# The second product of a two-layer squared-relu network by Strassen's seven products, on pairs of token chunks

## The chip, the cores and the metric

The kernel runs on one core of a Trainium2 chip. A core has five engines with their own instruction queues: TensorE (PE in the profile, its weight loads PEld), VectorE (DVE), ScalarE (ACT), GpSimd (POOL) and SyncE (SP), which here only issues transfers. TensorE writes to PSUM, and VectorE and ScalarE read it from there. The metric is the device time of one execution in microseconds.

## The reference, cut to what matters

```python
B, H, S, D = (4, 8, 768, 64)
for t in range(S):
    state = gamma * state + einsum('bhd,bhe->bhde', k[:, :, t], v[:, :, t])
    y[:, :, t] = scale * einsum('bhd,bhde->bhe', q[:, :, t], state)
x = y.transpose(0, 2, 1, 3).reshape(3072, 512)
h = np.maximum(x @ w_in, 0.0)          # w_in 512 x 2048
out = (h * h @ w_out).astype(np.float32)   # w_out 2048 x 512
```
A recurrent attention with one decay per head gives 3072 tokens of 512 values. A network with a hidden width of 2048 follows: a product, a relu, a square, a second product. Inputs and output are fp32 in memory; the products take bf16 operands and add up in fp32.

## The kernel before, in words

The 3072 tokens are 24 chunks of 128. The attention takes chunk after chunk; a "visit" on TensorE (lines 686 to 723) has the small products of one chunk, VectorE brings its result to `xt` (L788), and the state is added up by VectorE (L779). Inputs are loaded by SP in order (L616), k and q are cast by GpSimd for most chunks (L421), v is scaled on VectorE (L627), and from chunk 7 on q and k are transposed by a DMA (L660). Four load buffers, six bf16 buffers for k, q and v (`NBF`), six for the transposed q and k (`NQT`) and four groups of four chunks for x (`NXT`) stand between the steps.

The first product, `ffn1`, works on blocks of one, two or four chunks (`BLOCKS`). A group of matmuls fills one PSUM bank of 512 columns (L835): x moves and w_in is the stationary operand, so the moving width is 128 times the number of chunks of the block. A relu on ScalarE brings the bank to `h2` in bf16 (L840), and VectorE squares it there, in place (L845).

The second product, `ffn2`, takes one chunk at a time: 16 matmuls with 128x128 of `h2` as the stationary operand and 512 columns of w_out moving add up in one bank (L880), ScalarE copies the bank to `osb` (L888), and SP stores 256 KB (L893). The last chunk is cut into 256, 128 and 128 columns (`LAST`), the last of them stored from ScalarE's queue.

There are four PSUM banks (`fps`) for both products. Two of them at most may be held by open groups of the second product.

The order of all this is not written by hand. Each operation is added to a planner (`Plan`) with its engine, an expected duration, what it reads and writes, and a priority; the planner places at every step the operation that can start first, the lower priority number first among equals, and each engine then executes its own instructions in that fixed order. An operation given a choice of engines goes where it can start first. The hardware waits only for the semaphores that follow from what is read and written; an engine whose next instruction is not ready waits, even if a later one is. `HOME` pins some casts to an engine. The second product of a chunk is offered once the first product is four chunks ahead (`F2WAIT`), with a priority some chunks later (`F2LAG`):

```python
while done2 < done and blk0[done] - blk0[done2] >= F2WAIT:
    ffn2(done2)
    done2 += 1
```

Of the kernel before, what the change touches and what calls it, by code (L numbers as in the profile page):

```python
# [18 lines left out]
class Plan:  # L19
# [18 lines left out]
        self.lastw = {}  # L38
        self.readers = {}

    def add(self, name, eng, dur, reads=(), writes=(), fn=None, prio=0.0, lat=0.0, bank=None, after=(), count=0):
# [22 lines left out]
        self.ops.append(dict(i=i, name=name, eng=eng, flex=flex, deps=sorted(deps), fn=fn,  # L64
                             prio=prio, lat=lat, bank=bank, count=count))
        return i

    def schedule(self, nbanks, max_open):
        ops = self.ops
        n = len(ops)  # L70
        users = [[] for _ in range(n)]
# [15 lines left out]
        if "PE" in eng_free:  # L87
            eng_free["PE"] = 0.06 * PRE
        bank_free = [0.0] * nbanks
        bank_of = {}  # L90
        open_groups = set()
        closed = {}
# [6 lines left out]
        while done < n:  # L99
            best = None  # L100
            for eng, cand in pool.items():
                ef = eng_free[eng]
                for i in cand:
                    o = ops[i]
                    t = max(ef, ready_at[i])
                    b = o["bank"]
                    if b is not None and b[0] == "open":
                        if b[2] and len(open_groups) >= max_open:
                            continue
                        free = [x for x in bank_free if x is not None]  # L110
                        if not free:
# [85 lines left out]
                    open_groups.discard(b[1])  # L197
            if b is not None:
                o["bank_index"] = bank_of[b[1]]
            done += 1  # L200
            for u in users[i]:
                same = list(ops[u]["eng"]) == [eng] and not move
# [11 lines left out]
TURN = (0.60, 1.10, 16, 2.4)  # L214
WIDE = (0.60, 2.80, 33, 0.6)
STORE = (0.30, 0.80, 9, 0.6)
BLOCKS = [2, 2, 1, 1, 2, 2, 2, 2, 2, 4, 4]
SPLIT = 6
AHEAD = 4
WARM = 20.0  # L220
# [19 lines left out]
WPRIO = {"in": -2.0, "out": 2.0}  # L240


HOME = {'cq7': 'DVE', 'cwin1.0': 'ACT', 'Eq0.1': 'ACT', 'cwin5.2': 'POOL', 'Ek0.0': 'ACT', 'cwin4.1': 'DVE', 'ck0.1': 'POOL', 'Eq2.0': 'DVE', 'cq0.0': 'DVE', 'cwout3.1': 'ACT', 'Eq0.0': 'ACT', 'cwout2.1': 'ACT', 'cwin4.2': 'DVE', 'cwout2.2': 'ACT', 'cq5': 'POOL', 'cwin4.0': 'DVE', 'cwout3.0': 'DVE', 'cwin0.0': 'ACT', 'cwout0.3': 'POOL', 'cwout1.0': 'DVE', 'cwout2.3': 'POOL'}
ROUND = []
RANK = {}
# [13 lines left out]
def kernel(  # L259
# [29 lines left out]
    blk0 = [sum(blocks[:i]) for i in range(NB)]  # L289
    for x, n in zip(blk0, blocks):  # L290
        assert 512 % (n * C) == 0 and x // 4 == (x + n - 1) // 4
    NLD, NBF, NQT, NXT, NH2, NWS, NOSB, NST = 4, 6, 6, 4, 3, 4, 3, 6
    NBANK = 4

    const = ctx.enter_context(tc.tile_pool(name="const", bufs=1))
# [521 lines left out]
    def ffn1(blk):  # L817
        nb = blocks[blk]
        n = nb * C
        per = 512 // n  # L820
        g, u0 = divmod(blk0[blk], 4)
        xt, h2, cols = xts[g % NXT], h2s[g % NH2], slice(u0 * C, u0 * C + n)
        for f0 in range(0, NFB, per):
            grp = ("f1", blk, f0)
            j = f0 // 4
            reads = [f"xt{g % NXT}.{u0 + u}" for u in range(nb)] + [
                f"win{j}.{cb}.{h}" for cb in range(NCB) for h in sorted({(f0 + u) % 4 // 2 for u in range(per)})]
            o1 = {}

            def mm(f0=f0, j=j, o1=o1):  # L830
                ps = fps[o1["op"]["bank_index"]]
                for u in range(per):
                    c = (f0 + u) % 4
                    for cb in range(NCB):
                        nc.tensor.matmul(ps[:, u * n : u * n + n], lhsT=w_in_bf[j][:, cb, c * P : (c + 1) * P],  # L835
                                         rhs=xt[:, cb, cols], start=(cb == 0), stop=(cb == NCB - 1))

            def relu(f0=f0, o1=o1):
                ps = fps[o1["op"]["bank_index"]]
                nc.scalar.activation(h2[:, f0 : f0 + per, cols],  # L840
                                     ps[:].rearrange("p (u n) -> p u n", u=per), AF.Relu)

            def square(f0=f0):
                hv = h2[:, f0 : f0 + per, cols]
                nc.vector.tensor_mul(hv, hv, hv)  # L845

            i0 = pl.add(f"F1.{blk}.{f0}", "PE", per * NCB * (n * 0.4167 + 3) / 1e3, reads, (f"g{grp}",), mm,
                        prio=blk0[blk] * 8 + 2 * f0 * nb / 4, lat=0.2, bank=("open", grp, False),
                        count=per * NCB)
            o1["op"] = pl.ops[i0]  # L850
            hk = [f"h{g % NH2}.{u0 + w}.{f0 + u}" for u in range(per) for w in range(nb)]
            pl.add(f"R{blk}.{f0}", "ACT", 0.6, (f"g{grp}",), hk, relu,
                   prio=blk0[blk] + f0 / 16 * nb, bank=("close", grp),
                   after=twin_users if g == NH2 - 1 else pt_users if g == 1 else ())
            pl.add(f"Q{blk}.{f0}", "DVE", 0.43, hk, hk, square, prio=blk0[blk] + f0 / 16 * nb + 2)

    def rows(m):
        return where(m)[0] * S + where(m)[1] * C

    def ffn2(blk):  # L860
        for q4 in range(blk0[blk], blk0[blk] + blocks[blk]):
            g, u = divmod(q4, 4)
            h2 = h2s[g % NH2]
            slot = q4 % NOSB
# [34 lines left out]
    for kind in pieces:  # L899
        for n in range(len(pieces[kind])):  # L900
            weights(kind, n)
    done = done2 = 0
    for m in range(-1, NM):
        n = m + 1
# [12 lines left out]
            visit(m, n if n < NM else None, t)  # L917
        while done < NB and blk0[done] + blocks[done] - 1 == m:
            ffn1(done)
            while done2 < done and blk0[done] - blk0[done2] >= F2WAIT:  # L920
                ffn2(done2)
                done2 += 1
            done += 1
    for blk in range(done2, NB):
        ffn2(blk)

    sequence = pl.schedule(NBANK, 2)
    if tc is not None:
        with tc.manual_schedule():
            one = nc.const_aps.tensor(1.0, [P, 1], BF16)  # L930
# [39 lines left out]
```

## Time and profile before

| what | value |
|---|---|
| time, median of 3 runs | 209.82 us (209.39 to 210.51) |
| span of the profiled execution | 207.7 us; the page gives no other time for it |
| TensorE busy | 198.5 us, 96% |
| VectorE / ScalarE / GpSimd busy | 112.1 / 88.9 / 44.2 us |
| first product's matmuls, share of the chain | 41% |
| second product's matmuls, share of the chain | 39% |
| relu L840, 96 of them | 597 ns each |
| square L845, 96 of them | 448 ns mean |
| copy of the second product L888, 512 columns | 597 ns |

The page's span runs from the first to the last instruction; the time of a run is some 2 us longer. Busy times of different engines overlap. A line of the second part stands for 40 equal slices of the span, and a digit for tenths of a slice. The chain is followed back from the last instruction, and its shares add up to the span. In the lists of instructions a line gives the line of the code, the engine, the operation, what is written and read, and how often; some matmul records can be missing, so counts of matmuls come from the code. A matmul's own duration includes the way through the array and overlaps the next one, so its cost is read from the distance between starts.

### The profile page before, as it was taken

The numbers are of one execution on the slowest core, as the hardware profiler recorded it, in microseconds if no ns is written. First come the engines' busy times: TensorE is split into PE (matmuls) and PEld (weight loads), VectorE is DVE, ScalarE is ACT, GpSimd is POOL, SyncE is SP. The second block draws the span as 40 slices with busy tenths as digits, with TensorE's granted clock in tenths as the row PEclk, the third lists the DMA queues.
The fourth block names the chain that finished last, engine by engine and source line by source line (L and its number), as shares of the span: only waits on it lengthen the run. The fifth ranks groups of instructions, "written<-read, shape, count | busy, mean of one in ns | idle before, by whom it ended". The sixth has DMA issues, their size and how long they took to land.

```text
span 207.7 us, 6150 instructions
## 1 busy us (share of the span) xinstructions
PE 198.5 (96%) x2666; PEld 126.0 (61%) x2691; DVE 112.1 (54%) x245; ACT 88.9 (43%) x149; POOL 44.2 (21%) x75
## 2 busy tenths in 40 slices
PE   7898999999999999999999999999999999999994
PEld 5555797754854866868578666554444444444454
DVE  2597598753664574867558838436575414222000
ACT  8454576644321633535325252313643226344121
POOL 6643344342211122312212222112200000000000
PEclk9997999999999999999999999999999999999999
DMA  6999999999999999999999999989940111011112
GB/s 164 290 318 320 349 338 317 379 212 221 219 243 199 200 253 164 200 237 235 160 224 209 159 246 216 146 189 205 215 104 0 54 50 54 0 50 52 50 54 101
DMA packets 95643, 38.41 MB, mean 185 GB/s; under 512 B 81024, under 2 KB 89600, under 8 KB 95616
## 3 DMA queue, kind: packets, MB, share of 16 engines
q1 hardware_dynamic: 95472, 37.95, 86.3%
q8 instruction: 21, 0.34, 0.7%
q10 hardware_dynamic: 144, 0.07, 0.1%
q14 instruction: 6, 0.05, 0.1%
HBM read 27.26 MB, written 6.29 MB: 162 GB/s over the span
## 4 chain that ended last, share of the span: by engine, by line
PE 89%; DMA 4%; SPq 4%; issue 2%; ACT 0%
PE fps L835 41%; PE fps L880 39%; DMA wst<-in_moe_w_in_dram 4%; SPq L436 4%; PE yy L686 2%; PE yy L701 2%; PE sc L723 1%; PE sc L712 1%; PE fps L669 0%; ACT w_in L417 0%; PE sc L522 0%; PE sc L533 0%; PE yy L642 0%; PE yy L522 0%; PE yy L533 0%
## 5 line engine op out<-in xcount | busy, mean ns | idle before, releaser
L835 PE MATMUL fps<-xt,w_in 128*128 128x256 bf16 (+2 forms) x703 | 92.5, 284 | 1.0 <-ACT w_in L417 0.9
L880 PE MATMUL fps<-w_out,h 128*128 128x512 bf16 (+2 forms) x392 | 86.6, 362 | 2.5 <-issue 1.9
L840 ACT ACTIVATE h<-fps 128x512 bf16<-128x512 f32 x96 | 57.3, 597 | 60.3 <-PE fps L835 56.7
L835 PEld LDWEIGHTS <-w_in 128*128 128x128 bf16 x704 | 63.3, 98 | 25.2 <-ACT w_in L417 1.1
L845 DVE TENSOR_TENSOR h<-h 128x512 bf16<-128x512 bf16 x96 | 42.0, 448 | 48.0 <-ACT h L840 47.8
L880 PEld LDWEIGHTS <-h 128*128 128x128 bf16 x416 | 38.1, 98 | 37.4
L888 ACT ACTIVATE osb<-fps 128x512 f32<-128x512 f32 (+2 forms) x26 | 14.7, 564 | 46.4 <-PE fps L880 43.5
L421 POOL CAST kqs<-kn 128x512 bf16<-128x512 f32 x20 | 13.2, 658 | 61.7 <-DMA kn<-in_k_dram 60.2
L788 DVE TENSOR_TENSOR xt<-yy,yf 128x512 bf16<-128x512 f32 x20 | 13.7, 686 | 15.0 <-PE yy L701 15.0
L627 DVE TENSOR_TENSOR vs<-vn,vf 128x512 bf16<-128x512 f32 x20 | 14.5, 727 | 6.2 <-DMA vn<-in_v_dram 6.2
L421 POOL CAST kqs<-qn 128x512 bf16<-128x512 f32 x19 | 12.8, 673 | 21.4 <-DMA qn<-in_q_dram 21.4
L779 DVE TENSOR_TENSOR state<-sc,state 128x256 bf16<-128x256 f32 x33 | 13.8, 418 | 0.6
L766 DVE TENSOR_TENSOR pt<-sc,cmask 128x512 bf16<-128x512 f32 x20 | 13.6, 680 | 0.3 <-PE sc L723 0.3
L701 PE MATMUL yy<-qkT,state 64*64 64x64 bf16 x296 | 9.9, 198 | 0.2
L686 PEld LDWEIGHTS <-vs 64*64 64x64 bf16 x320 | 4.2, 107 | 7.0 <-issue 6.6
L936 PE MATMUL fps<-ident 128*128 128x256 bf16 x31 | 7.3, 377 | 0.3 <-POOL ident L352 0.3
L421 POOL CAST w_in<-wst 128x512 bf16<-128x512 f32 x7 | 4.7, 681 | 8.9 <-DMA wst<-in_moe_w_in_dram 8.9
L686 PE MATMUL yy<-pt,vs 64*64 64x64 bf16 x320 | 6.4, 198 | 0.0
L701 PEld LDWEIGHTS <-state 64*64 64x64 bf16 x296 | 6.1, 107 | 0.4 <-PE yy L701 0.4
L723 PE MATMUL sc<-vs,kqs 64*64 64x64 bf16 x288 | 6.2, 193 | 0.0
L712 PE MATMUL sc<-qkT 64*64 64x64 bf16 x320 | 6.2, 193 | 0.0
L421 POOL CAST w_out<-wst 128x512 bf16<-128x512 f32 x7 | 4.4, 653 | 7.6 <-DMA wst<-in_moe_w_out_dram 7.6
(67 smaller groups left out, 85.0 us busy)
## 6 DMA issues: line engine op xcount, KB each, us to landing
out_dram<-osb SPq DMA_DIRECT2D x23, 256.0 KB, 3.7
qn<-in_q_dram SPq DMA_DIRECT2D x20, 256.0 KB, 5.0
kn<-in_k_dram SPq DMA_DIRECT2D x20, 256.0 KB, 5.1
vn<-in_v_dram SPq DMA_DIRECT2D x20, 256.0 KB, 4.9
wst<-in_moe_w_out_dram SPq DMA_DIRECT2D x4, 1024.0 KB, 10.1
wst<-in_moe_w_in_dram SPq DMA_DIRECT2D x4, 512.0 KB, 8.7
wst<-in_moe_w_in_dram SPq DMA_DIRECT2D x2, 1024.0 KB, 8.8
kn<-in_k_dram SPq DMA_DIRECT2D x2, 512.0 KB, 5.7
```

Source lines behind the costliest of these rows:

```text
L421: nc.gpsimd.tensor_copy(o, t)
L627: lambda: nc.vector.tensor_tensor(out=o[:], in0=t.rearrange("s (h d) -> s h d", h=H), in1=vf[:, i, :, None].to_broadcast([P, H, D]), op=AL ...
L686: nc.tensor.matmul(yy[L * c : L * c + L, sub, p * L : p * L + L], lhsT=vs[r, 4 * a + j, :], rhs=pt[r, a, j, :], start=(p == 0), stop=True, ...
L701: nc.tensor.matmul(yy[L * c : L * c + L, sub, p * L : p * L + L], lhsT=st[r, j, :], rhs=qkT[r, 1, j, sub * L : sub * L + L], start=False, ...
L766: lambda: nc.vector.tensor_tensor(out=pt[:], in0=sc[:, :, 0:256].rearrange("s g (p t) -> s g p t", p=NJ), in1=cmask[:, None, None, :].to_b ...
L779: f = lambda cc=cc, j1=j1, j0=j0: nc.vector.tensor_tensor(out=sts[j1][:], in0=cc, in1=sts[j0][:], op=ALU.add)
L788: lambda: nc.vector.tensor_tensor(out=xt[:, :, u * C : u * C + C].rearrange("s p (g t) -> s g p t", g=2), in0=yy[:, :, 0:256].rearrange("s ...
L835: nc.tensor.matmul(ps[:, u * n : u * n + n], lhsT=w_in_bf[j][:, cb, c * P : (c + 1) * P], rhs=xt[:, cb, cols], start=(cb == 0), stop=(cb = ...
L840: nc.scalar.activation(h2[:, f0 : f0 + per, cols], ps[:].rearrange("p (u n) -> p u n", u=per), AF.Relu)
L845: nc.vector.tensor_mul(hv, hv, hv)
L880: nc.tensor.matmul(ps[:, 0:w], lhsT=h2[:, fb, u * C : u * C + C], rhs=w_out_bf[j][:, c, ns], start=(fb == 0), stop=(fb == NFB - 1))
L888: lambda o1=o1, slot=slot, ns=ns, w=w: nc.scalar.activation(osbs[slot][:, ns], fps[o1["op"]["bank_index"]][:, 0:w], AF.Copy),
```

## The change

From chunk 4 on the second product works on pairs of chunks. With A the pair's squared h cut into 2 x 2 blocks (rows: the two chunks; columns: halves of the hidden width) and B = w_out cut into 2 x 2 (halves of the hidden width; 256 output columns each), the seven products of Strassen's rule stand in place of eight:

- M1 = (A11 + A22)(B11 + B22), M2 = (A21 + A22) B11, M3 = A11 (B12 - B22), M4 = A22 (B21 - B11), M5 = (A11 + A12) B22, M6 = (A21 - A11)(B11 + B12), M7 = (A12 - A22)(B21 + B22)
- C11 = M1 + M4 - M5 + M7, C12 = M3 + M5, C21 = M2 + M4, C22 = M1 - M2 + M3 + M6

Each product is eight matmuls of 256 columns. The order on TensorE is 3, 4, 1, 5, 2, 6, 7, in two PSUM banks A and B. The five sums of A (S1, S5, S2, S6, S7, 128x1024 in bf16) are made by VectorE; S6 and S7 overwrite blocks of `h2`, the others lie in the buffers where the weights were staged. The sums of B (T1, T3, T4, T6, T7, ten halves) are made once, by VectorE or GpSimd, in the same buffers. After products 3 and 4 ScalarE copies bank A (`e34`), which gives M3 and M4; products 5 and 2 then add to that bank, which gives C12 and C21, and ScalarE copies it again (`cc`). ScalarE copies M1 out of bank B (`e1`). Three additions in fp32, by GpSimd or VectorE (`t1`, `u1`, `w`), bring these together, and one addition by VectorE with bank B (`c`) gives C11 and C22. SP issues two stores of 256 KB for a pair.

The relu now writes fp32 into one of two buffers (`rts`, `NR`), and the square reads it there and writes bf16 to `h2`, on VectorE or ScalarE, whichever can start first; the planner has the two buffers as slots. `BLOCKS` has twos where it ended with two fours. `NBF` and `NQT` go from six to five, `NXT` from four to three. Chunks 0 to 3 keep the second product as it was; the split of the last chunk isn't met any more, since `UNTIL` is 24. In the planner the two new arguments `slot` and `nslots` do for the relu buffers what `bank` does for PSUM banks.

```diff
--- before.py
+++ after.py
...
-BLOCKS = [2, 2, 1, 1, 2, 2, 2, 2, 2, 4, 4]
+BLOCKS = [2, 2, 1, 1, 2, 2, 2, 2, 2, 2, 2, 2, 2]
...
+SQUARE = {"DVE": 0.7, "ACT": 0.63}
+WSUM = {"DVE": 0.72, "POOL": 2.6}
+ASUM = {"DVE": 0.72}
+FADD = {"POOL": 0.75, "DVE": 0.43}
+FADD2 = {"POOL": 1.3, "DVE": 0.7}
+FIRST, UNTIL = 4, 24
+PAIRS_B = {"T1": ((0, 0), (1, 1), ALU.add), "T3": ((0, 1), (1, 1), ALU.subtract), "T4": ((1, 0), (0, 0), ALU.subtract),
+           "T6": ((0, 0), (0, 1), ALU.add), "T7": ((1, 0), (1, 1), ALU.add)}
+PAIRS_A = {"S1": ((0, 0), (1, 1), ALU.add, None), "S5": ((0, 0), (0, 1), ALU.add, None),
+           "S2": ((1, 0), (1, 1), ALU.add, None), "S6": ((1, 0), (0, 0), ALU.subtract, (1, 0)),
+           "S7": ((0, 1), (1, 1), ALU.subtract, (0, 1))}
...
-    NLD, NBF, NQT, NXT, NH2, NWS, NOSB, NST = 4, 6, 6, 4, 3, 4, 3, 6
+    NLD, NBF, NQT, NXT, NH2, NWS, NOSB, NST = 4, 5, 5, 3, 3, 4, 3, 6
+    NR, NUN = 2, 2
...
+    rts = [sb(f"r{j}", [P, 512], FP32) for j in range(NR)]
+    e34s = [sb(f"e34{j}", [P, 512], FP32) for j in range(NUN)]
+    ccs = [osbs[j] for j in range(2)]
+    wus = [osbs[2], sb("wu", [P, DM], FP32)]
+    half_slots = [wst[j][:].rearrange("p a n -> p (a n)").bitcast(BF16).rearrange("p (s c n) -> p s c n", s=4, c=4)
+                  for j in range(4)]
...
-            def relu(f0=f0, o1=o1):
-                ps = fps[o1["op"]["bank_index"]]
-                nc.scalar.activation(h2[:, f0 : f0 + per, cols],
-                                     ps[:].rearrange("p (u n) -> p u n", u=per), AF.Relu)
-
-            def square(f0=f0):
-                hv = h2[:, f0 : f0 + per, cols]
-                nc.vector.tensor_mul(hv, hv, hv)
+
+            def relu(o1=o1):
+                nc.scalar.activation(rts[o1["relu"]["slot_index"]][:], fps[o1["op"]["bank_index"]][:], AF.Relu)
+
+            def square(on, f0=f0, o1=o1):
+                hv, rv = h2[:, f0 : f0 + per, cols], rts[o1["relu"]["slot_index"]][:].rearrange("p (u n) -> p u n", u=per)
+                if on == "ACT":
+                    nc.scalar.activation(hv, rv, AF.Square)
+                else:
+                    (nc.vector if on == "DVE" else nc.gpsimd).tensor_tensor(out=hv, in0=rv, in1=rv, op=ALU.mult)
 
...
-            pl.add(f"R{blk}.{f0}", "ACT", 0.6, (f"g{grp}",), hk, relu,
-                   prio=blk0[blk] + f0 / 16 * nb, bank=("close", grp),
+            i0 = pl.add(f"R{blk}.{f0}", "ACT", 0.6, (f"g{grp}",), (f"r{grp}",), relu,
+                        prio=blk0[blk] + f0 / 16 * nb, bank=("close", grp), slot=("open", grp))
+            o1["relu"] = pl.ops[i0]
+            pl.add(f"Q{blk}.{f0}", SQUARE, 0, (f"r{grp}",), hk, square, prio=blk0[blk] + f0 / 16 * nb + 2, slot=("close", grp),
                    after=twin_users if g == NH2 - 1 else pt_users if g == 1 else ())
-            pl.add(f"Q{blk}.{f0}", "DVE", 0.43, hk, hk, square, prio=blk0[blk] + f0 / 16 * nb + 2)
 
...
+    def sums_of_weights():
+        slot = [0]
+
+        def place():
+            j, s = divmod(slot[0], 4)
+            slot[0] += 1
+            return half_slots[j][:, s], [f"wst{j}.0", f"wst{j}.1"]
+        made = {}
+        for name, (x, y, op) in PAIRS_B.items():
+            for half in range(2):
+                t, held = place()
+                blocks_ = [w_out_bf[2 * r + half][:, :, 256 * c : 256 * c + 256] for r, c in (x, y)]
+                reads = [f"wout{2 * r + half}.{c}.{h}" for r, _ in (x, y) for c in range(4) for h in range(2)]
+                pl.add(f"W{name}.{half}", WSUM, 0, reads, [f"T{name}.{half}"] + held,
+                       lambda on, t=t, blocks_=blocks_, op=op: (nc.vector if on == "DVE" else nc.gpsimd).tensor_tensor(
+                           out=t, in0=blocks_[0], in1=blocks_[1], op=op), prio=3.0)
+                made[name, half] = (t, f"T{name}.{half}")
+        sums = {}
+        for j in range(NUN):
+            for name in ("S1", "S2", "S5"):
+                t, held = place()
+                sums[name, j] = (t.rearrange("p c (e n) -> p (c e) n", e=2), held)
+        return made, sums
+
+    def products(c0):
+        n = units_made[0]
+        units_made[0] += 1
+        g, u = divmod(c0, 4)
+        h2 = h2s[g % NH2]
+        z = n % NUN
+        a = {(r, c): h2[:, 8 * c : 8 * c + 8, (u + r) * C : (u + r + 1) * C] for r in range(2) for c in range(2)}
+        key = {(r, c): [f"h{g % NH2}.{u + r}.{f}" for f in range(8 * c, 8 * c + 8)] for r in range(2) for c in range(2)}
+        for name, (x, y, op, dst) in PAIRS_A.items():
+            if dst is None:
+                a[name], held = asums[name, z]
+                key[name] = [f"{name}.{z}"]
+            else:
+                a[name], held, key[name] = a[dst], [], key[dst]
+            pl.add(f"{name}.{c0}", ASUM, 0, key[x] + key[y], key[name] + held,
+                   lambda on, o=a[name], x=a[x], y=a[y], op=op: (nc.vector if on == "DVE" else nc.gpsimd).tensor_tensor(
+                       out=o, in0=x, in1=y, op=op), prio=c0 + 1.5)
+        wb = lambda r, c, f: w_out_bf[2 * r + f // 4][:, f % 4, 256 * c : 256 * c + 256]
+        bkey = lambda r: [f"wout{2 * r + x}.{c}.{h}" for x in range(2) for c in range(4) for h in range(2)]
+        tb = lambda name, f: wsums[name, f // 4][0][:, f % 4]
+        tkey = lambda name: [wsums[name, x][1] for x in range(2)]
+        PRODUCTS = {
+            1: ("S1", lambda f: tb("T1", f), tkey("T1")),
+            2: ("S2", lambda f: wb(0, 0, f), bkey(0)),
+            3: ((0, 0), lambda f: tb("T3", f), tkey("T3")),
+            4: ((1, 1), lambda f: tb("T4", f), tkey("T4")),
+            5: ("S5", lambda f: wb(1, 1, f), bkey(1)),
+            6: ("S6", lambda f: tb("T6", f), tkey("T6")),
+            7: ("S7", lambda f: tb("T7", f), tkey("T7")),
+        }
+        opened, count = {}, [0]
+
+        def product(i, bank, half, bank_use):
+            left, right, reads = PRODUCTS[i]
+            first = bank not in opened
+            op = opened.setdefault(bank, {})
+
+            def mm():
+                ps = fps[op["op"]["bank_index"]]
+                for f in range(8):
+                    nc.tensor.matmul(ps[:, 256 * half : 256 * half + 256], lhsT=a[left][:, f], rhs=right(f),
+                                     start=(first and f == 0), stop=True, skip_group_check=True)
+            k = pl.add(f"M{i}.{c0}", "PE", 0.877, key[left] + reads, (f"gS{c0}{bank}",), mm,
+                       prio=(c0 + 1 + F2LAG) * 8 + count[0] * 16 / 7, lat=0.2,
+                       bank=(bank_use, ("s", c0, bank), True) if bank_use == "open" else (bank_use, ("s", c0, bank)), count=8)
+            count[0] += 1
+            if first:
+                op["op"] = pl.ops[k]
+
+        def read(name, eng, dur, bank, reads, writes, fn, close=False, prio=0.0):
+            pl.add(f"{name}.{c0}", eng, dur, [f"gS{c0}{bank}"] + list(reads), writes,
+                   lambda: fn(fps[opened[bank]["op"]["bank_index"]]), prio=c0 + 1 + prio,
+                   bank=("close", ("s", c0, bank)) if close else ("use", ("s", c0, bank)))
+
+        e34, cc, wu = e34s[z], ccs[z], wus[z]
+        kcc, kwu = OSB[z], OSB[2 + z]
+        product(3, "A", 0, "open")
+        product(4, "A", 1, "use")
+        read("e34", "ACT", 0.6, "A", (), (f"e34{z}",), lambda ps: nc.scalar.activation(e34[:], ps[:], AF.Copy))
+        product(1, "B", 0, "open")
+        read("e1", "ACT", 0.36, "B", (), kwu, lambda ps: nc.scalar.activation(wu[:, 256:512], ps[:, 0:256], AF.Copy))
+        pool = lambda o, x, y, op: (lambda on: (nc.vector if on == "DVE" else nc.gpsimd).tensor_tensor(out=o, in0=x, in1=y, op=op))
+        pl.add(f"t1.{c0}", FADD, 0, [f"e34{z}"] + kwu, kwu, pool(wu[:, 0:256], e34[:, 0:256], e34[:, 256:512], ALU.add), prio=c0 + 1)
+        pl.add(f"u1.{c0}", FADD, 0, kwu, kwu, pool(wu[:, 256:512], wu[:, 0:256], wu[:, 256:512], ALU.add), prio=c0 + 1)
+        product(5, "A", 0, "use")
+        product(2, "A", 1, "use")
+        read("cc", "ACT", 0.6, "A", (), kcc, lambda ps: nc.scalar.activation(cc[:], ps[:], AF.Copy), close=True)
+        pl.add(f"w.{c0}", FADD2, 0, kcc + kwu, kwu, pool(wu[:], wu[:], cc[:], ALU.subtract), prio=c0 + 1)
+        product(6, "B", 1, "use")
+        product(7, "B", 0, "use")
+        read("c", "DVE", 0.69, "B", kwu, kwu,
+             lambda ps: nc.vector.tensor_tensor(out=wu[:], in0=ps[:], in1=wu[:], op=ALU.add), close=True)
+        for t, k, x in ((cc, kcc, 1), (wu, kwu, 0)):
+            dst = bass.AP(out.tensor, rows(c0) * DM + 256 * x, [[DM, P], [C * DM + (256 if x == 0 else -256), 2], [1, 256]])
+            pl.add(f"st{c0}.{x}", "SP", STORE, k, (),
+                   lambda t=t, dst=dst: nc.sync.dma_start(dst, t[:].rearrange("p (i n) -> p i n", i=2)), prio=-1)
+
+    OSB = [[f"osb{s}.{y}" for y in range(len(LAST))] for s in range(3)] + [["wu"]]
+
+    def ffn2(c0, n):
+        for q4 in range(c0, c0 + n):
...
+    wsums, asums = sums_of_weights()
+    units_made = [0]
+
+    def finish(c0):
+        if FIRST <= c0 < UNTIL:
+            products(c0)
+        else:
+            ffn2(c0, 2)
+
...
-            while done2 < done and blk0[done] - blk0[done2] >= F2WAIT:
-                ffn2(done2)
-                done2 += 1
+            while done2 < NM and done2 + 2 <= blk0[done] and blk0[done] - done2 >= F2WAIT:
+                finish(done2)
+                done2 += 2
             done += 1
-    for blk in range(done2, NB):
-        ffn2(blk)
-
-    sequence = pl.schedule(NBANK, 2)
+    while done2 < NM:
+        finish(done2)
+        done2 += 2
+
+    sequence = pl.schedule(NBANK, 2, NR)
```

More of the change, by code (lines that the diff above doesn't have):

```diff
@@ L39, in __init__, with add @@
         self.readers = {}
-    def add(self, name, eng, dur, reads=(), writes=(), fn=None, prio=0.0, lat=0.0, bank=None, after=(), count=0):
+    def add(self, name, eng, dur, reads=(), writes=(), fn=None, prio=0.0, lat=0.0, bank=None, after=(), count=0, slot=None):
         i = len(self.ops)
@@ L64, in add, with schedule @@
         self.ops.append(dict(i=i, name=name, eng=eng, flex=flex, deps=sorted(deps), fn=fn,
-                             prio=prio, lat=lat, bank=bank, count=count))
+                             prio=prio, lat=lat, bank=bank, count=count, slot=slot))
         return i
-    def schedule(self, nbanks, max_open):
+    def schedule(self, nbanks, max_open, nslots):
         ops = self.ops
@@ L89, in schedule @@
         bank_free = [0.0] * nbanks
+        slot_free = [0.0] * nslots
+        slot_of = {}
         bank_of = {}
@@ L110, in schedule @@
                         free = [x for x in bank_free if x is not None]
+                        if not free:
+                            continue
+                        t = max(t, min(free))
+                    if o["slot"] is not None and o["slot"][0] == "open":
+                        free = [x for x in slot_free if x is not None]
                         if not free:
@@ L199, in schedule @@
                 o["bank_index"] = bank_of[b[1]]
+            if o["slot"] is not None:
+                if o["slot"][0] == "open":
+                    k = min((x, j) for j, x in enumerate(slot_free) if x is not None)[1]
+                    slot_free[k], slot_of[o["slot"][1]] = None, k
+                    o["slot_index"] = k
+                else:
+                    slot_free[slot_of[o["slot"][1]]] = end[i] + self.HOP
             done += 1
@@ L854, in ffn1 @@
                    after=twin_users if g == NH2 - 1 else pt_users if g == 1 else ())
-            pl.add(f"Q{blk}.{f0}", "DVE", 0.43, hk, hk, square, prio=blk0[blk] + f0 / 16 * nb + 2)
     def rows(m):
         return where(m)[0] * S + where(m)[1] * C
-    def ffn2(blk):
-        for q4 in range(blk0[blk], blk0[blk] + blocks[blk]):
+    def sums_of_weights():
[20 more added lines that the diff above has]
+        return made, sums
@@ L901 @@
             weights(kind, n)
+    wsums, asums = sums_of_weights()
[3 more added lines that the diff above has]
+            products(c0)
+        else:
+            ffn2(c0, 2)
     done = done2 = 0
```

## The prediction, written before the changed kernel was run

> **What bounds the kernel now.** I read the page's busy table and slices first, then the chain that ended last in order of time, then single lines with their shortest, middle and longest duration, then the busy time by stretches, and last the end of the timeline.
>
> ```profile
> span 207.7 us, 6150 instructions
> PE 198.5 (96%) x2666; PEld 126.0 (61%) x2691; DVE 112.1 (54%) x245; ACT 88.9 (43%) x149; POOL 44.2 (21%) x75
> PE   7898999999999999999999999999999999999994
> DVE  2597598753664574867558838436575414222000
> DMA  6999999999999999999999999989940111011112
> PE 89%; DMA 4%; SPq 4%; issue 2%; ACT 0%
> ```
> TensorE is the bound: full in every slice but the first few and the last, and 89% of the chain is its own work. VectorE is nearly as full only in the slices around 25 to 40 us.
>
> ```profile
> 23.73 5.24 PE fps L835 x48
> 54.14 3.57 PE fps L835 x64
> 170.24 6.04 PE fps L835 x28
> ```
> In the chain (start, length, what) back-to-back matmuls of one width give the pace: 256 columns 5.24/48 = 109.2 ns, 128 columns 3.57/64 = 55.8 ns, 512 columns 6.04/28 = 215.7 ns (four of L880 take 0.864, 216 each). So a matmul costs its columns and some 2 ns more.
>
> ```profile
> 20.00:40.00 20.00, 19.78 (x266) 16.41 (x268) 16.29 (x33) 13.32 (x23) 8.50 (x13) 0.97 1.09 344
> 40.00:60.00 20.00, 19.58 (x326) 12.45 (x329) 10.03 (x21) 8.47 (x15) 5.46 (x8) 1.00 1.09 233
> 60.00:100.00 40.00, 39.31 (x625) 28.47 (x627) 26.85 (x56) 16.25 (x28) 9.18 (x14) 1.00 1.26 212
> 100.00:150.00 50.00, 49.10 (x714) 30.22 (x722) 29.71 (x62) 18.55 (x32) 10.64 (x16) 1.00 1.14 199
> 150.00:192.00 42.00, 41.39 (x392) 19.67 (x391) 16.66 (x37) 17.41 (x30) 0.00 (x0) 1.00 0.15 47
> ```
> Stretches; the columns are length, then busy time of PE, PE weight loads, DVE, ACT, POOL, then clock, DMA share, GB/s. PE idles 2.6 us of the 172 from 20 to 192; the engines that feed it have room on average, least in 20 to 40.
>
> ```profile
> L845 DVE TENSOR_TENSOR h<-h x96: 407/425/830, 19.9 to 192.5; 128x512 bf16<-128x512 bf16 x96
> L627 DVE TENSOR_TENSOR vs<-vn,vf x20: 678/684/1103, 30.9 to 153.2; 128x512 bf16<-128x512 f32 x20
> L421 POOL CAST kqs<-kn x20: 616/616/964, 26.6 to 148.1; 128x512 bf16<-128x512 f32 x20
> L452 POOL TENSOR_TENSOR h<-vn,vf x2: 1043/1295/1547, 8.7 to 14.1; 128x512 bf16<-128x512 f32 x2
> ```
> Durations min/median/max. A square costs 425 ns in bf16; the fp32 product L627 costs 684. The long maxima are met only where DVE and POOL run together.
>
> ```profile
> 204.89 0.28 ACT L888 ACTIVATE osb<-fps 128x128 f32<-128x128 f32 x1 [0.61 <-PE fps L880]
> 205.19 0.37 ACTq L893 DMA_DIRECT2D out_dram<-osb  x1
> ```
> The timeline's end: the last matmul ends at 204.85, a 0.28 copy and a 64 KB store follow, landing 1.6 later (206.8), and the span closes 0.9 after that.
>
> **The change, part by part.** The profiled execution has a span of 207.7; the median of the three times is 209.82. The 2.1 outside the span is taken as unchanged, so differences go straight onto the median. Half a percent, about 1.05 us, is what a measurement here can tell from no change.
>
> Products. A pair of chunks was 2 x 16 matmuls of 512 columns: 32 x 216.1 = 6.92. It becomes 7 x 8 of 256: 56 x 109.2 = 6.12. Ten pairs (chunks 4 to 23) save 8.0. Weight loads go from 32 to 56 per pair, 98 ns each, under a pace of 109: L835 has just this shape and runs at it, so they cost nothing; with that cover gone it would be 98 x 24 = 2.4 per pair. BLOCKS cuts the last two blocks from four chunks to two: 128 matmuls of 512 become 256 of 256, 27.96 - 27.66 = +0.30. Chunk 23's split into 256, 128 and 128 columns goes: 16 x 109.2 + 32 x 55.8 = 3.53 against 3.46, -0.08. Net on TensorE: **-7.78**, all on its path.
>
> End. After the last product a 128x512 add on DVE from PSUM (0.684, the L788 row's median), then a 256 KB store through SP, in pieces of 1 KB where 2 KB stood. Late stores in the quiet end land in 1.6 to 4.0, median 2.0. So 0.04 + 0.68 + 0.05 + 2.0 + 0.9 = 3.7 against 2.85 now; **+0.9**, with 2.9 for a store as slow as the slowest. It also needs w (below) done; the products 6 and 7 cover it with 1.75, against copy 0.6 + POOL add 1.3 = 1.9.
>
> Squares in fp32. Each of 96 goes from 425 to 684 ns on DVE, or 621 (L417, ACT from SBUF) on ACT. Relu itself stays 0.6, but writes into one of only two fp32 buffers, and its PSUM bank is freed as before while the next relu must wait for a square two groups back. A buffer is held for 0.6 + 0.03 + 0.69 + 0.03 = 1.35, so two give a group each 0.68; TensorE makes one each 0.874. That fits while each square finds an engine free. One DVE instruction of 0.42 to 0.69 ahead of it makes 1.8 to 2.04, 0.9 to 1.02 a group: up to 0.15 late, and behind the waiting relu on ACT stand the evacuations, so the PSUM banks fill and TensorE waits.
> In 20 to 40 there are 17 squares in TensorE's unmixed F1 run (no second product exists yet to fill in): +17 x 0.26 = 4.4 on DVE gives 20.7 of 20. Five moved to ACT give DVE 17.3, ACT 16.4: it fits on average, not in order. Bounds: 0 (all hidden) and 17 x 0.2 = 3.4 plus 0.6 for one late weight cast, 4.0. I take 0.1 a group, **+1.7**, nearest to the row that DVE already had 0.2 to 0.3 between squares only.
>
> Sums of h. Five per pair, 128x1024 bf16. From L845 (425 at 512) and the slope 0.533 that 684 and 418 (L779, 256 wide) imply at half rate, 152 + 546 = 0.70; at full rate 1.22. I take 0.70, the rate that L845 shows for two bf16 inputs: 3.5 a pair, 35 in all. The closing add: 6.9. ACT: 0.597 + 0.384 + 0.597 against 2 x 0.597, +0.38 a pair. POOL: two 256-wide and one 512-wide fp32 adds, about 0.7, 0.7, 1.3, 27 in all. Weight sums: ten, 0.7 on DVE in bf16, 7.0, or 2 to 3 each on POOL (twice the L452 row); the last w_out cast ends near 45 us and pair 4 is needed near 60, where DVE has 10 of 20 free. Covered; if not, the pair's 6.1 starts that much later.
> From 60 to 192 DVE has 73.2 of 132 and ACT 52.2. Adding 35, 6.9, 71 x 0.26 = 18.5: DVE 133.6, over the stretch. With 40 squares on ACT: DVE 106 (80%), ACT 52.2 + 3.8 + 24.8 = 81 (61%). It fits, with TensorE now at the mercy of order: product 1 needs the first sum, product 5 needs the 0.6 copy of the bank (0.16 + 0.6 + 0.06 against 0.874 of product 1, covered by 0.05).
> What lateness costs there is in no row. Below: 0; a gain is excluded, since PE idles only 2.6 us over 20 to 192. Above: the squares and the casts overshoot their medians now by 96 x 0.023 + 20 x 0.043 + 39 x 0.05 = 5.0 us over 53 POOL instructions, 0.09 each. Thirty POOL adds half again as long, against 1.7 times the DVE work, give 0.24 x 30 + 0.07 x 53, about 10 more. I take a quarter, **+2.5**, since now next to nothing of those 5 reaches TensorE and the slack is halved.
>
> Buffers (x 3, casts 5, qkT 5): the last transposes start at 149.8, three to four visits ahead of their use, so five slots still cover it; x of group g now waits for F1 of g-3, done some 40 us earlier. Nothing; if the cover is gone, a late visit lets the other work on TensorE go first until the backlog (50 us after the loads end at 150) is used. A store queued on SP behind a late closing add would hold loads up; the same backlog covers it. The first pair's 0.8 may be lost, as TensorE has little in hand near 66 us; it is inside the 2.5.
>
> Sum: 209.82 - 7.78 + 0.95 + 1.7 + 2.5 = **207.2**.
>
> **A rule against it.** SBUF — State Buffer, Who interferes with whom, in the Trainium skill: a VectorE instruction with two SBUF inputs and a GpSimd instruction that reads SBUF exclude each other for a whole instruction. The maxima above agree (830 is 425 plus most of a 616 cast). By it the 27 us of POOL adds and the 35 of sums take turns; without it the 2.5 would be near 0.5 and the sum 205.2.
>
> **The rivals.** (1) All of it is covered: -7.78 + 0.95 gives 203.0. For: 20% of DVE and 39% of ACT free. Against: two relu buffers.
> (2) DVE and POOL hold each other up and half of the 10 us reaches TensorE: 207.2 - 2.5 + 5.0 = 209.7, no change. For: the maxima; against: casts and squares collide now and TensorE doesn't wait.
> (3) Slower: the relu buffers become the bound of F1. Net of the end the change has 6.8 to lose; over 88 groups (17 + 71) that is 78 ns a group. From there on it decides. If two groups in three wait 0.15 to 0.2, 88 x 2/3 x 0.17 = 10, and 203.0 + 10 = 213. For: one DVE instruction ahead of a square is enough. Against: F1 groups mostly alternate with second products, so two buffers have 1.75 a group.
>
> **How the numbers follow.** The forecast's case has 0.37 (205 to 208.7 its own range), (1) 0.19, (2) 0.15, (3) 0.29. Faster is the first two, 0.56; same (2), 0.15; slower (3), 0.29. The range leaves out about 0.07 below 202.8 and 0.1 above 214.
>
> **What would show it.** Matmuls of L880's successor at 109 ns in runs of eight; L835 without 512-wide forms; squares near 0.69 on DVE and 0.62 on ACT in about equal numbers; sums near 0.70 (at 1.2 DVE would be full, and I am wrong by far). Waits of TensorE for ACT or DVE of about 4 us more than now, half of them before 40 us; above 10, rival (3), with ACT's relus waiting for squares. The end after the last matmul 3.7 long.

## The result and the profile after

The changed kernel takes 212.97 us (211.55 to 213.72, four runs) against 210.16 (209.39 to 211.10, four runs): 1.0133 times the time before, with a 95% interval of 1.0084 to 1.0182. It is slower, where 207.2 and faster was forecast. Its profiled execution took 213.18 with a span of 211.4, 3.7 more than the span before.

First the page's busy table, slices and chain, then the busy time by stretches (length, then PE, PE weight loads, DVE, ACT, POOL, then clock, DMA share, GB/s), of the changed kernel.

```profile
span 211.4 us, 7033 instructions
PE 194.4 (92%) x3027; PEld 159.4 (75%) x3027; DVE 158.2 (75%) x260; ACT 125.7 (59%) x219; POOL 77.1 (36%) x98
PE   7697999898299997989999999999999999999991
PEclk9999999999889999999999999999999999999998
PE 52%; DMA 24%; SPq 10%; DVE 7%; POOL 2%; issue 2%; ACT 1%; POOLq 1%; ACTq 0%
```
```profile
20.00:40.00 20.00, 19.03 (x261) 15.37 (x259) 15.38 (x26) 16.44 (x30) 9.45 (x13) 1.00 1.10 344
40.00:60.00 20.00, 15.49 (x201) 8.31 (x200) 18.55 (x21) 9.06 (x15) 12.91 (x8) 0.91 1.00 227
60.00:100.00 40.00, 37.89 (x693) 32.14 (x691) 30.05 (x49) 22.37 (x40) 11.32 (x14) 1.00 1.00 166
100.00:150.00 50.00, 49.49 (x886) 43.02 (x884) 44.67 (x72) 34.75 (x63) 16.96 (x22) 1.00 1.30 198
150.00:192.00 42.00, 41.92 (x576) 36.83 (x574) 29.50 (x48) 27.14 (x47) 9.03 (x11) 1.00 0.39 85
```
TensorE no longer carries 89% of the chain but 52%. The hole is the eleventh slice of the busy row (a 2); in that slice and the next the clock row has an 8: in 40 to 60 us TensorE was busy for 15.5 us where it had been for 19.6. VectorE was busy for 18.55 there, and GpSimd for 12.9 where it had been for 5.5. From 100 to 192 us TensorE idles 0.6 us of 92, less than before (1.5), although VectorE is busy there for 60% longer (74.2 us against 46.4).

What fills the hole, in the order of time: VectorE, then GpSimd, then TensorE, from 42 us on.

```profile
42.35 0.69 DVE L909 TENSOR_TENSOR wst<-w_out,w_out 128x1024 bf16<-128x1024 bf16 x1 [1.06 <-POOL w_out L453]
42.95 2.61 DVE L909 TENSOR_TENSOR wst<-w_out 128x1024 bf16<-128x1024 bf16 x1
...
47.10 2.61 DVE L659 TENSOR_TENSOR vs<-vn,vf 128x512 bf16<-128x512 f32 x1
49.63 2.60 DVE L909 TENSOR_TENSOR wst<-w_out,w_out 128x1024 bf16<-128x1024 bf16 x1
52.16 2.60 DVE L909 TENSOR_TENSOR wst<-w_out 128x1024 bf16<-128x1024 bf16 x1
54.68 0.68 DVE L659 TENSOR_TENSOR vs<-vn,vf 128x512 bf16<-128x512 f32 x1
55.28 0.68 DVE L909 TENSOR_TENSOR wst<-w_out,w_out 128x1024 bf16<-128x1024 bf16 x1
55.89 0.68 DVE L798 TENSOR_TENSOR pt<-sc,cmask 128x512 bf16<-128x512 f32 x1
```
```profile
42.39 2.62 POOL L909 TENSOR_TENSOR wst<-w_out,w_out 128x1024 bf16<-128x1024 bf16 x1
46.72 2.44 POOL L909 TENSOR_TENSOR wst<-w_out,w_out 128x1024 bf16<-128x1024 bf16 x1 [1.70 <-DVE w_out L451]
49.12 5.09 POOL L909 TENSOR_TENSOR wst<-w_out 128x1024 bf16<-128x1024 bf16 x2
```
```profile
56.62 0.43 PE L718 MATMUL yy<-pt,vs 64*64 64x64 bf16 x16 [3.85 <-DVE pt L798]
57.73 2.98 PE L1018 MATMUL fps<-w_out,h 128*128 128x512 bf16 x8
60.55 1.61 PE L867 MATMUL fps<-xt,w_in 128*128 128x128 bf16 x26
```
L909 is the sums of w_out, made once: six on VectorE, four on GpSimd. A sum takes 0.68 on VectorE alone. Each VectorE instruction with two SBUF inputs that starts while GpSimd sums ends 0.55 us after GpSimd's sum ends: 42.39 + 2.62 = 45.01, and VectorE's second sum ends at 45.56. Four instructions take 2.6 instead of 0.68, among them a scaling of v (L659). The engines seem to take turns, for GpSimd's sums are held up as well: each began while such an instruction of VectorE was under way. The first began 0.65 us before that instruction ended, the second 0.46; 2.62 - 0.65 and 2.44 - 0.46 both give 2.0, which is an estimate of what a sum takes on GpSimd alone. No run has one alone. Behind them in VectorE's fixed order stands the masking of the scores (L798), for which TensorE waits 3.85 us. When it goes on, eight matmuls of 512 columns take 2.92 (365 ns each in place of 216). TensorE comes to the first product of chunk 5 at 60.55; before, after the same work, it was there at 53.98:

```profile
53.98 3.74 PE L835 MATMUL fps<-xt,w_in 128*128 128x128 bf16 x64
```
At 43 us both kernels were at the same place (43.07 and 42.98). So **6.6 us were lost** here.

The rest of the account: from there to the last matmul's end (204.85 before, 207.05 after) 146.5 us in place of 150.9, 4.4 saved of 7.78; waits for transposed q and k, 1.2 at 84 us, 0.9 at 93 and 0.5 at 138, are 2.6 of the difference. From the last matmul to the span's end it is 4.35 in place of 2.85. Together +6.6 - 4.4 + 1.5 = +3.7.

### The profile page after: what moved, and what is told of

Same layout as the page of the kernel before. It is cut to its first block, busy times and chain, and to the rows that moved or that the text cites. A ratio compares the mean times of both kernels' runs of the same rounds, so it can differ in the third digit from the quotient of the medians.

```text
span 211.4 us, 7033 instructions
## 1 busy us (share of the span) xinstructions
PE 194.4 (92%) x3027; PEld 159.4 (75%) x3027; DVE 158.2 (75%) x260; ACT 125.7 (59%) x219; POOL 77.1 (36%) x98
## 4 chain that ended last, share of the span: by engine, by line
PE 52%; DMA 24%; SPq 10%; DVE 7%; POOL 2%; issue 2%; ACT 1%; POOLq 1%; ACTq 0%
PE fps L867 23%; PE fps L959 23%; DMA kn<-in_k_dram 11%; DMA qkT<-kqs 6%; DMA wst<-in_moe_w_out_dram 5%; DVE wst L909 4%; SPq L841 4%; SPq L648 3%; PE fps L1018 2%; DMA out_dram<-osb 2%; SPq L468 2%; DVE vs L659 2%; PE yy L718 1%; PE sc L744 1%; SPq L692 1%
## 5 line engine op out<-in xcount | busy, mean ns | idle before, releaser
L867 PE MATMUL fps<-xt,w_in 128*128 128x256 bf16 (+1 forms) x832 | 92.6, 265 | 1.2 <-ACT w_in L449 1.1
L872 ACT ACTIVATE r<-fps 128x512 f32<-128x512 f32 x96 | 56.2, 591 | 38.5 <-PE fps L867 35.0
L879 DVE TENSOR_TENSOR h<-r 128x512 bf16<-128x512 f32 x37 | 28.1, 761 | 17.8 <-ACT r L872 17.6
L959 PE MATMUL fps<-wst,h 128*128 128x256 bf16 x320 | 39.4, 273 | 0.0
L877 ACT ACTIVATE h<-r 128x512 bf16<-128x512 f32 x59 | 36.5, 628 | 1.4
L959 PEld LDWEIGHTS <-wst 128*128 128x128 bf16 x240 | 23.2, 98 | 2.8
L934 DVE TENSOR_TENSOR wst<-h 128x1024 bf16<-128x1024 bf16 x30 | 21.4, 746 | 0.9 <-ACT h L877 0.6
L959 PE MATMUL fps<-w_out,wst 128*128 128x256 bf16 x160 | 20.2, 273 | 0.0
L659 DVE TENSOR_TENSOR vs<-vn,vf 128x512 bf16<-128x512 f32 x20 | 17.0, 856 | 3.5 <-DMA vn<-in_v_dram 3.5
L934 DVE TENSOR_TENSOR h<-h 128x1024 bf16<-128x1024 bf16 x20 | 16.4, 853 | 0.3
L1018 PE MATMUL fps<-w_out,h 128*128 128x512 bf16 x64 | 16.2, 400 | 0.1
L798 DVE TENSOR_TENSOR pt<-sc,cmask 128x512 bf16<-128x512 f32 x20 | 13.6, 680 | 0.3 <-PE sc L755 0.3
```

What stands on the lines that cost most here:

```text
L659: lambda: nc.vector.tensor_tensor(out=o[:], in0=t.rearrange("s (h d) -> s h d", h=H), in1=vf[:, i, :, None].to_broadcast([P, H, D]), op=AL ...
L798: lambda: nc.vector.tensor_tensor(out=pt[:], in0=sc[:, :, 0:256].rearrange("s g (p t) -> s g p t", p=NJ), in1=cmask[:, None, None, :].to_b ...
L872: nc.scalar.activation(rts[o1["relu"]["slot_index"]][:], fps[o1["op"]["bank_index"]][:], AF.Relu)
L877: nc.scalar.activation(hv, rv, AF.Square)
L879: (nc.vector if on == "DVE" else nc.gpsimd).tensor_tensor(out=hv, in0=rv, in1=rv, op=ALU.mult)
L934: lambda on, o=a[name], x=a[x], y=a[y], op=op: (nc.vector if on == "DVE" else nc.gpsimd).tensor_tensor(out=o, in0=x, in1=y, op=op), prio=c ...
```

## The experiments

Theory "lock": GpSimd's sums, which read SBUF, keep VectorE's two-input instructions from running, and nothing else in the change costs much. Rivals: VectorE is simply overfull there; GpSimd's time hurts, since its casts come late; the two fp32 relu buffers throttle the first product (the slower rival of the prediction). Each run was compared with the kernel before on its own chip, and the time of that kernel differs by up to 0.6 us between the chips (209.54 to 210.16). So differences between two runs are taken from their ratios below, times 209.8.

**GpSimd fills in place of sums, all else in its place**

```diff
-    lambda on, ...: (nc.vector if on == "DVE" else nc.gpsimd).tensor_tensor(out=t, in0=blocks_[0], in1=blocks_[1], op=op)
+    lambda on, ...: nc.gpsimd.memset(t, 0.0) if on == "POOL" else nc.vector.tensor_tensor(out=t, in0=blocks_[0], in1=blocks_[1], op=op)
```

> The changed kernel with every instruction in its place, but the weight sums that fall to GpSimd are fills that write the same buffer and read nothing (so four of the ten weight sums are left out and the output is not the reference's). Theory lock: the 6.5 us that TensorE lost between 43 and 60 us come from GpSimd's weight sums (2.5 us each), which keep VectorE's instructions with two SBUF inputs from running. Then VectorE's weight sums and v scalings take 0.7 each here, TensorE's wait of 3.9 us for the masked scores goes, and the time is 206 to 208. Rival, VectorE overfull: it has more work there than it can do whatever GpSimd does; then the wait stays over 2.5 us and the time is 211 to 213.

206.23 us, ratio 0.9843 (0.9810 to 0.9877). The same order of instructions is 6.1 us faster than the changed kernel by the two ratios, and TensorE no longer waits for the masked scores. But a fill is also shorter, 0.95 against 2.5, so the next run keeps GpSimd occupied.

**Each fill three times**

```diff
+    lambda on, ...: [nc.gpsimd.memset(t, 0.0) for _ in range(3)] if on == "POOL" else nc.vector.tensor_tensor(...)
```

> As the run with fills, but each fill is done three times, so that GpSimd is occupied about as long as with its four sums (some 2.8 us each) and still reads nothing (four of the ten weight sums are left out). Theory lock (only a GpSimd instruction that reads SBUF holds VectorE up): as with the single fills, 205.5 to 207, and VectorE's weight sums stay at 0.7. Rival: it is GpSimd's time that hurts, its casts of q and k coming late; then 211 to 213.

206.26 us, ratio 0.9824 (0.9793 to 0.9854). The timeline of GpSimd, and VectorE's sums (duration min/median/max; they are line 910 here):

```profile
41.97 12.45 POOL L909 MEMSET wst<- 128x1024 bf16 x12
55.68 0.61 POOL L453 CAST kqs<-qn 128x512 bf16<-128x512 f32 x1 [1.26 <-DMA qn<-in_q_dram]
```
```profile
L910 DVE TENSOR_TENSOR wst<-w_out,w_out x4: 675/679/691, 42.1 to 51.0; 128x1024 bf16<-128x1024 bf16 x4
L910 DVE TENSOR_TENSOR wst<-w_out x2: 679/682/685, 42.7 to 48.3; 128x1024 bf16<-128x1024 bf16 x2
```
GpSimd is occupied from 41.97 to 54.4 without a pause (in the changed kernel from 42.39 to 54.21 with one pause of 1.70), and VectorE's sums take 0.68 all the same. So neither GpSimd's time nor VectorE's load is the cause, but what GpSimd does in that time: a sum, which reads SBUF, holds VectorE's two-input instructions up, and a fill, which reads nothing, does not. SBUF — State Buffer in the Trainium skill, Who interferes with whom, has this rule, with instructions that only write excepted, and the runs agree with both halves of it.

**All weight sums on VectorE**

```diff
-WSUM = {"DVE": 0.72, "POOL": 2.6}
+WSUM = {"DVE": 0.72}
```

> All ten weight sums on VectorE (the choice of GpSimd is taken from the planner). Theory lock: ten sums at 0.7 each, no VectorE instruction of 2.6 left, TensorE's idle time from 40 to 60 us falls from 4.5 to under 1.5 and the time is 207 to 209. Rival, VectorE overfull: four more sums on the busiest engine make it worse, 213 to 216.

205.49 us (205.39 to 205.61), ratio 0.9812 (0.9793 to 0.9831): nothing is left out here, and it is faster than both kernels, and than the 207 to 209 that were expected. The stretch and the sums:

```profile
40.00:60.00 20.00, 19.52 (x277) 12.46 (x279) 16.49 (x26) 10.56 (x19) 5.94 (x9) 1.00 1.08 239
60.00:100.00 40.00, 38.65 (x728) 33.15 (x726) 36.34 (x57) 25.41 (x48) 11.90 (x15) 1.00 1.19 207
```
```profile
L909 DVE TENSOR_TENSOR wst<-w_out,w_out x6: 676/684/1123, 42.1 to 48.7; 128x1024 bf16<-128x1024 bf16 x6
L909 DVE TENSOR_TENSOR wst<-w_out x4: 674/680/1092, 43.4 to 51.4; 128x1024 bf16<-128x1024 bf16 x4
```
VectorE makes ten sums instead of six and is busy for 16.5 us there instead of 18.55. TensorE idles 0.5 of the 20 us, and its clock stays at 1.00.

**No weight sums**

```diff
-    blocks_ = ...
-    reads = ...
-    pl.add(f"W{name}.{half}", WSUM, 0, reads, [f"T{name}.{half}"] + held, ...)
-    made[name, half] = (t, f"T{name}.{half}")
+    made[name, half] = (w_out_bf[half][:, :, 0:256], f"wout{half}.3.0")
```

> No weight sums at all: the five products that need one read a block of w_out in its place (so the output is not the reference's). Theory: on VectorE alone the ten sums are covered, so leaving them out gains at most 1 us on the 205.5 of that run, 204.5 to 205.5. Rival: seven us on a full engine still cost 2 or more, 203.5 or less.

206.36 us, ratio 0.9844 (0.9808 to 0.9880): no faster than with ten sums on VectorE, and outside both expectations. The order of the rest changed too (TensorE waits 2.9 us for transposed q and k, which the run before did not), so this shows that the sums cost nothing that another order doesn't, not that they cost nothing.

**The parts around the products alone**

```diff
-FIRST, UNTIL = 4, 24
+FIRST, UNTIL = 24, 24
-    wsums, asums = sums_of_weights()
```

> The change without Strassen's products: fp32 relu in two buffers, squares on VectorE or ScalarE, blocks of two chunks at the end, fewer x, q, k buffers; no weight sums. Theory lock (these parts are cheap): 209.8 plus 0.3 for the narrower last blocks plus about 1 for late squares, 210 to 211.5. Rival, relu buffers: the two buffers throttle the first product, 78 ns or more a group, 215 or more.

209.89 us against 209.54, ratio 1.0032 (1.0008 to 1.0057). Fp32 relu in two buffers, squares on two engines, narrower last blocks and fewer buffers cost 0.35 us together by the medians and 0.7 by the ratio; the narrower blocks alone were worked out at 0.30. That is a little less than expected, and far from the rival's 215: the two relu buffers by themselves are not what made the change slower.

**Squares in bf16 as before, with Strassen's products and all weight sums on VectorE**

```diff
-    pl.add(f"Q{blk}.{f0}", SQUARE, 0, (f"r{grp}",), hk, square, ..., slot=("close", grp), ...)
+    pl.add(f"Q{blk}.{f0}", "DVE", 0.43, hk, hk, square, prio=blk0[blk] + f0 / 16 * nb + 2)
```
with relu into `h2` and the in-place square of the kernel before.

> All weight sums on VectorE, Strassen's products, but relu and square as before the change: bf16 into the h buffer, squared in place by VectorE, no relu buffers. Rival of the prediction, relu buffers: the two fp32 buffers still cost TensorE several us beside the sums, so this is 200 to 203.5. Theory (they are covered also beside the sums): within 1 us of the 205.5 with fp32 squares, 204.5 to 206.5; VectorE gets all 96 squares at 0.43.

208.69 us, ratio 0.9930 (0.9900 to 0.9960): by the ratios 2.5 us slower than with fp32 squares. Both expectations missed, the rival's by sign. The stretch and TensorE's longest wait in that run:

```profile
100.00:150.00 50.00, 47.31 (x861) 40.50 (x860) 49.07 (x90) 21.49 (x38) 16.86 (x21) 1.00 1.11 193
```
```profile
PE fps L867 <- DVE xt L820: 2.6, 3, 1.7
```
With all squares on VectorE it is busy for 49.07 of 50 us, and TensorE waits for x, which VectorE writes. In the changed kernel 59 of 96 squares went to ScalarE. The changed kernel's squares differ in two things, the fp32 buffer that they read and the choice of engine, and together these are worth 2.5 us beside Strassen's sums. That it is the choice is likely, from VectorE's load, but not shown: bf16 squares in place with the same choice of engine were not run.

**The three additions of a pair on VectorE**, once with the weight sums as in the changed kernel and once with them on VectorE:

```diff
-FADD = {"POOL": 0.75, "DVE": 0.43}
-FADD2 = {"POOL": 1.3, "DVE": 0.7}
+FADD = {"DVE": 0.43}
+FADD2 = {"DVE": 0.7}
```

> The three fp32 additions of a pair only on VectorE; weight sums as in the changed kernel. Theory queue (a second, smaller loss: the additions stand ahead of the k and q casts on GpSimd, so transposed q and k come late around 84 and 93 us, 2.2 us in all, and at the end the last addition takes 1.3): 213 - 2 - 0.6, 210 to 211. Rival, the additions hide on GpSimd and VectorE needs its time for the sums: 213 to 216.

211.61 us, ratio 1.0111 (1.0069 to 1.0152), against 1.0133 (1.0084 to 1.0182) of the changed kernel: the intervals overlap, so no gain is shown, and both expectations missed. The waits for transposed q and k are gone (TensorE is busy for 39.64 of 40 us from 60 to 100), and the hole at 56 us is as it was. That the additions hold casts up on GpSimd fits this: in the changed kernel GpSimd sat idle for 9.68 us, until 69.2, before the first of them.

> All weight sums and all three additions of a pair on VectorE. Theory as in the prediction (GpSimd's additions delay VectorE's sums and this reaches TensorE with some 2 us): 203 to 204.5. Rival: after 60 us TensorE has cover for that, and VectorE's extra 15 us make it worse: 205.5 to 208.

207.74 us, ratio 0.9898 (0.9865 to 0.9931): by the ratios 1.8 slower than with the additions on GpSimd, in the rival's range; it was expected to gain. So the same edit takes the waits for q and k away in one order and costs time in the other, where TensorE waits 2.0 us for x and 1.9 for q and k. Which of the two effects rules in general stays open.

**The end**

```diff
-FIRST, UNTIL = 4, 24
+FIRST, UNTIL = 4, 22
```
with all weight sums on VectorE.

> All weight sums on VectorE, and the last two chunks by the old second product with its split at the end. TensorE has 0.8 us more to do, the way from the last matmul to the end falls from 4.3 to 2.9: 204.5 to 205.3. Rival: the last pair's length is covered by nothing that gets shorter, or the new order loses more than it gains: 206 or more.

205.57 us, ratio 0.9800 (0.9773 to 0.9828): not to be told from 0.9812 with the pair, and between the two expectations. The way from the last matmul (200.6) to the span's end (203.5) is 2.9, as expected, but that matmul is 1.3 later instead of 0.8. The granted clock of the first 20 us was 0.83 in this profile and 1.00 in that of the kernel altered, so part of the 1.3 may come from there.

```diff
-    pl.add(f"w.{c0}", FADD2, 0, ...)
+    pl.add(f"w.{c0}", FADD2 if c0 + 2 < UNTIL else {"DVE": 0.7}, 0, ...)
```
and the same for `t1` and `u1`, with all weight sums on VectorE.

> All weight sums on VectorE, and the three additions of the last pair alone on VectorE; order of the rest unchanged. The closing addition need no longer wait for GpSimd (0.33 us after the last product in the changed kernel): 0.3 to 0.5 less than 205.5, 205.0 to 205.3. Rival: the end is bound by the last product, 205.4 to 205.7.

206.56 us, ratio 0.9863 (0.9801 to 0.9924); the interval holds the 0.9812 of the kernel that it alters, so nothing is shown of the 0.3 to 0.5 that were expected. The closing addition now starts 0.04 after the last matmul (200.47), yet the store behind it starts 0.42 after the addition ends, and the end is as long as before. Here too the first 20 us had a clock of 0.83 in place of 1.00, so the spans aren't compared.

## Why the prediction was wrong, point by point

The step that failed is the sentence on the weight sums: "Covered; if not, the pair's 6.1 starts that much later". It priced a sum at 0.7 on VectorE or 2 to 3 on GpSimd and found 10 of VectorE's 20 us free. The prices lay in these bounds (0.68, and 2.44 to 2.62). But the planner used both engines at once, and side by side an instruction on VectorE lasts as long as GpSimd's sum and its own together: 2.6 in place of 0.68, four times. Nor was the first pair what waited: it was the attention's masking, queued behind the sums on VectorE. TensorE lost 6.6 us there, for which the forecast had nothing; with fills in the place of GpSimd's sums the change is 6.1 us faster, which is more than its whole loss.

The rule that explains it was quoted, and was held against the additions of a pair, where the prediction saw 27 us of GpSimd. It was not held against the weight sums, where GpSimd has four of them within 12 us, and VectorE six instructions with two inputs in the same time.

**Products, -7.78.** Borne out as a price: in the changed kernel's chain a run of 112 products' matmuls takes 12.30, 109.8 ns each against 109.2. What the gain is worth to TensorE's end can't be read more closely than the waits that lie between.

**End, +0.95.** Measured +1.5, inside the bound that the prediction gave (the sum for its slowest store would be 2.9). Its own parts give 3.67 - 2.85 = 0.82; the text has 0.9 and the sum 0.95. The closing addition began 0.37 after the last product in place of 0.04, since GpSimd's addition was late, as 1.9 against 1.75 had warned; the store with what follows took 3.3 in place of 2.95.

**Squares before 40 us, +1.7.** TensorE idled 0.97 there against 0.22, 0.75 of it until a square of ScalarE was done. That it was at the same place at 43 us as before doesn't make the term zero, because it had a lead:

```profile
22.35 5.62 PE L867 MATMUL fps<-xt,w_in 128*128 128x256 bf16 x48
```
```profile
23.56 5.40 PE L835 MATMUL fps<-xt,w_in 128*128 128x256 bf16 x48
```
The kernel before came to this run (the second line) 1.2 us later: its granted clock was 0.50 from 18 to 20 us, where the changed kernel's was 1.00. At 43 us the lead was gone (43.07 against 42.98), so 1.3 us were lost on the way: 0.4 in this run and the 32 matmuls behind it, and most of the rest in the wait of 0.77 at 39.3. Three other runs with a clock of 1.00 in the first 20 us (the triple fills, no weight sums, all additions on VectorE) wait as long there, but for a cast of q, so a late square need not be what the wait cost. The run of these parts alone bounds the term better: 0.35 to 0.7 with the narrower blocks, so 1.7 was too much. ScalarE's relus waited for VectorE's squares 1.9 us in all; most squares, 59, went to ScalarE at 0.63, into the same queue as the relus.

**Lateness after 60 us, +2.5.** The overshoot was sized about rightly. Over the span the 50 sums of h, 37 squares and 20 scalings of v are above their medians of 0.68 to 0.69 by 30 x 0.066 + 20 x 0.173 + 37 x 0.07 + 20 x 0.17 = 11.4 us, and the 32 casts of k and q on GpSimd by 3.2; 1.9 of it is the scaling among the weight sums. The other 12.7 are 7.7 more than the 5.0 before, where about 10 was worked out. From 100 to 192 us TensorE idles 0.6 in all. Some 2.6 us did reach it by a way that the prediction had put at nothing: additions ahead of casts in GpSimd's order, so that transposed q and k were late (with the additions on VectorE, in the run above, these waits were gone). That 2.6 is close to the 2.5 of the term is luck. The "backlog" meant to cover it exists only later; near 66 us TensorE had little in hand, as the prediction itself had noted. The prediction's 2.6 us of idle TensorE from 20 to 192 us add up to 2.8 in its own table; nothing rests on it.

**The rivals.** The slower one has the right time, 213, by luck, for its mechanism is wrong: in the changed kernel ScalarE's relus wait for squares of VectorE 1.9 us in all, and 35.0 us for TensorE. The full gain of 203.0 is not reached by any run; the best is 205.49.

## What to carry to other kernels

Where a planner or a table gives an operation a choice between VectorE and GpSimd, add up the two engines' two-input work as if it were on one engine: the summary row of each shows it free, but while both read SBUF they took turns here, and an instruction of 0.68 lasted 2.6. Work that is "made once" needs the same reading as work in the loop: look up the stretch in which it falls, what stands behind it in each engine's queue, and who waits for that. Leaving a cheap operation the choice of a second engine can be worth more than a faster format on the fuller one; here the two together made 2.5 us, and they were not separated.

## What the runs showed of the hardware that was not expected

A VectorE instruction's duration in the profile includes the time for which it is held up: 2.6 us for a sum of 0.68, with VectorE "busy" all the while. Of the 18.55 us of 20 (93%) for which it was busy from 40 to 60, 4 x 1.93 = 7.7 were waiting.

Fills on GpSimd, which leave VectorE's sums alone, do slow VectorE's casts from SBUF to SBUF: three of 128x512 took 2.94 us during the fills and 1.09 with GpSimd idle in the changed kernel. SBUF — State Buffer in the Trainium skill, Who interferes with whom, says that casts can take both of VectorE's ports and contend with GpSimd; here that is seen on a GpSimd instruction that only writes.

TensorE's clock fell after a wait of 3.85 us: the granted clock was 0.91 over 40 to 60 us, in it 0.64 from 56 to 58 and 0.51 from 58 to 60, and the eight matmuls behind the wait took 365 ns each. The shorter waits around 84 and 93 us, 1.2 and 0.9, left it at 1.00. TensorE: Matmul & The Clock Gate in the Trainium skill, Part 1, gives some 3.4 us of idleness as what it takes, and these waits lie on both sides of that. But a single long wait is not the only way there: in the kernel before the clock fell to 0.50 at 18 to 20 us, though no wait of TensorE from 8 to 18 us was over 0.9, and in the changed kernel it stayed at 1.00 in that stretch. Why is not shown. The wait of 3.85 cost about a third more than its length (2.92 - 1.73 = 1.2 on the eight matmuls alone).
